# A sliding-window attention layer with a gated FFN on one core: two of four token blocks transposed through DRAM and VectorE, FFN tiles placed between the QKV blocks

## The chip, the cores and the metric

The kernel runs on one core of a Trainium2 chip. The metric is the device time of one execution in microseconds (us); for the kernel before it is 230.87 us, the median of 3 runs (230.71 to 231.08). All times below come from one profiled execution of that kernel, which took 230.75 us, and whose recorded span from the first to the last instruction is 229.0 us.

## The reference

```python
def reference(A_x, A_wqkv, A_wo, B_x, B_w_gate, B_w_up, B_w_down):
    x = A_x                                  # 1 x 2048 x 512, bf16
    xn = _layernorm(x, axis=-1)              # no scale, no shift
    s = _A_ref(xn, A_wqkv, A_wo)             # attention: 32 heads of 16; each token sees 8 keys,
                                             # its own and those 2, 4, ... 14 tokens back; then @ wo
    g = _silu(_B_ref(xn, B_w_gate, B_w_up, B_w_down))   # (gelu(xn @ w_gate) * (xn @ w_up)) @ w_down
    return x + s * g                         # FFN width 1792
```

## The kernel before

The 2048 tokens are 16 tiles of 128, in four blocks j of 512 (TQ). Everything stays on chip except V, which is written to DRAM transposed (`vT_dram`) and read back with shifted windows (`v_arr`). For each block the work is:

- `layer_norm` (L296 on): BatchNorm statistics on VectorE (L303, L304), the root on ScalarE (blocks 0 and 1, L310) or on GpSimd (blocks 2 and 3, L325 and L328), the normalised tile `xn_t` on VectorE (L335). `transpose` (L346 on) then turns each tile with four 128x128 TensorE transposes into PSUM (L351) and copies them to `xnT` (L359 on ScalarE, L361 on VectorE). `xnT` has the channels on the partitions and the tokens in a row: it is the moving operand of all that follows.
- `qkv` (L410 on): q, k and v, each four groups of four 128x512 matmuls over the channels (L430; block 0 in matmuls of 256 columns), evacuated by ScalarE (L443, L449, L454). The weights of q and k are read with a step of four elements.
- `scores` (L505 on): for each half w2 of the window, four products q * k on VectorE of 128x2048 (L517) and two pairwise sums (L527), then eight matmuls of 32 columns that sum over the head's channels (`L_ps`, L534), the exponential on ScalarE (L546), and the normaliser (`sum_ps` L588, reciprocal L598, `b_ps` L606).
- `values` (L623 on): the same on the V side (L639, L649, `O_ps` L656, `o_sb` L667).
- `ffn_pair` (L705 on), 14 a block: four matmuls for the gate and four for the up projection (both L710), gelu on ScalarE (L720), the product `hT` on VectorE (L727), which frees the bank of `u_ps`.
- `out_tile` (L744 on), 4 a block: 4 matmuls with wo (`s_ps`, L752), 14 with w_down (`y_ps`, L764), silu (L775), gate (L778), residual (L785), store (L789). The very last tile is cut only for the s part, in 384 and 128 columns.

The order on each engine is written by a small planner, the class `Order` (L45 to L151). Every piece of work is a task with an engine, an assumed duration (the constants L26 to L38), a priority, and the buffers that it takes and frees. `run` takes at each step the task that can start first, and emits it. The TensorE matmuls of qkv, ffn_pair and out_tile are one chain in the order of the loops at the end of the kernel (`add_main`, L391): all four qkv blocks, and then for each block 14 pairs and 4 output tiles. Transposes, score, sum and value matmuls go between them when their inputs are planned to be there.[...]

PSUM has four banks for the main chain (pool `psf`), two for transposes, scores and normalisers (`psa`) and one pair for `O_ps` (`pso`).

The loads are issued by SP (x, wqkv, in the order L195 to L216) and by ScalarE (w_gate, w_up, wo, w_down at L844, each behind a named task); the windows of V by GpSimd (L496).[...] `wqkv_sb` shares its buffer with the hidden tile `hT`.

Of the kernel before, what the change touches and what calls it, by code (L numbers as in the profile page):

```python
# [9 lines left out]
ALU = mybir.AluOpType  # L10
# [4 lines left out]
P = 128  # L15
# [9 lines left out]

MM = 0.216  # L26
COL16 = 1.1
COL8 = 0.65
TR = 0.28
PROD = 1.14  # L30
HMUL = 0.6
STATS = 0.8
NORM = 0.36
TRCOPY = 0.36
ACT1 = 0.62
ACT2 = 1.06
TABLE = 1.28
HOP = 0.2  # L38
# [6 lines left out]
class Order:  # L45
# [45 lines left out]
    def run(self):  # L91
        left = list(self.tasks)
        while left:
# [10 lines left out]
            if t.eng == "dve" and t.prio >= 1.0:  # L104
                soon = [
                    (self.ready(u), u.seq, u) for u in left
                    if u.eng == "dve" and u.prio <= -1.5 and self.ready(u) is not None
                ]
                if soon and min(soon)[0] < s + 0.4:
                    s, _, t = min(soon)  # L110
# [20 lines left out]
def kernel(  # L131
# [23 lines left out]
    def pool(name, bufs, **kw):  # L155
# [9 lines left out]
    prpool = pool("prpool", 6)  # L165
# [6 lines left out]
    psf = pool("psf", 4, space=bass.MemoryType.PSUM)  # L172
    psa = pool("psa", 2, space=bass.MemoryType.PSUM)
# [5 lines left out]
        {"xn": 4, "q": 3, "vst": 4, "va": 3, "pr": 6, "attn": 2, "o": 2, "h": 1, "gl": 3, "sg": 3,  # L179
         "f": 4, "a": 2, "O": 1}  # L180
# [5 lines left out]
    wqkv_sb = hpool.tile([P, 3, NC * D + 64], BF16, name="wqkv_sb", tag="h")  # L186
    order.taken["h"].append("wqkv")
# [3 lines left out]
    wd_sb = wpool.tile([P, NF, D], BF16, name="wd_sb")  # L191
    wqkv_v = A_wqkv.rearrange("(k p) n -> p k n", p=P)

    for t in range(TPB):
        eng = nc.sync if t % 2 == 0 else nc.scalar  # L195
        eng.dma_start(out=x_sb[:, t, :], in_=x2d[t * P : (t + 1) * P, :])  # L196
# [12 lines left out]
    load_wqkv(0)  # L209
# [6 lines left out]
    x_there = [3.2, 3.5, 3.8, 4.1] + [9.5] * 2 + [12.0] * 2 + [13.5] * 4 + [16.0] * 4  # L216
# [58 lines left out]
    xnT = cpool.tile([P, NC, S], BF16, name="xnT")  # L275
# [20 lines left out]
    def layer_norm(j):  # L296
# [49 lines left out]
        def transpose(t, dep, on_act):  # L346
            def fn():
                tiles["tr", t] = psa.tile([P, NC * P], BF16, name="tr_ps", tag="a")
                for c in range(NC):
                    cs = slice(c * P, (c + 1) * P)  # L350
                    nc.tensor.transpose(tiles["tr", t][:, cs], tiles["xn", t][:, cs], ident[:])  # L351
                if t < 2:
                    warm_up(2 + t, TQ // 2)
# [9 lines left out]
            a = add("pe", TR, fn, deps=[dep], prio=-1.0, takes=[("a", ("tr", t))], frees=[("xn", t)])  # L363
# [3 lines left out]
            )  # L367

# [8 lines left out]
        elif j == 1:  # L377
# [5 lines left out]
        else:  # L383
            r = rstd_done[j] = rstd_pool(ts[0], TPB, [stat(t) for t in ts])
            for t in ts:
                transpose(t, norm(t, r), on_act=False)
# [10 lines left out]
    v_stored = {}  # L397

# [11 lines left out]
    def qkv(j):  # L410
# [4 lines left out]
        for lo in range(0, TQ, n):  # L415
            for which in range(3):
                for c in range(0, NC, w):
                    key = (j, which, c, lo)

                    def mms(key=key, which=which, c=c, lo=lo):  # L420
                        ps = psf.tile([P, TQ], F32, name="qkv_ps", tag="f")
                        tiles["qkv", key] = ps
                        for i in range(w):
                            for dk in range(NC):
# [3 lines left out]
                                else:  # L428
# [4 lines left out]
                                    rhs=xnT[:, dk, j * TQ + lo : j * TQ + lo + n],  # L433
# [41 lines left out]
                    else:  # L475
                        st = add("sp", 0.6, store_v(j, c, lo, n, w), deps=[e], prio=-1.0)

                        v_stored[j] = add(
                            ("dma", key), 3.0, lambda: None, deps=[(st, 0.0)], frees=[("vst", key)]
# [5 lines left out]
    def load_values(j, half):  # L485
# [12 lines left out]
        issue = add("pool", 2.4, fn, deps=[v_stored[j]], prio=-2.0, takes=[("va", (j, half))])  # L498
        v_ready[j, half] = add(("dma", "va", j, half), 7.5, lambda: None, deps=[(issue, 0.0)])
# [5 lines left out]
    def scores(j, prio):  # L505
        exps = []
        for w2 in range(2):
# [21 lines left out]
            def reduce(w2=w2, prods=prods):  # L529
                L = psa.tile([P, TQ], F32, name="L_ps", tag="a")  # L530
                tiles["L", j, w2] = L
                for i in range(2):
                    for w4 in range(4):
# [5 lines left out]
                            stop=(i == 1),  # L539
# [14 lines left out]
            for c in range(NC):  # L554
# [9 lines left out]
                if c % 2 == 1:  # L564
# [3 lines left out]
                            opens=key, closes=key if last else None, frees=[("pr", (*key, c))],  # L568
                        )
                    )  # L570
            r = add(
                "pe", COL8, reduce, deps=[ps[-1]], prio=-0.5, takes=[("a", ("L", j, w2))],
                frees=[("pr", (*key, c)) for c in (0, 2)],
# [44 lines left out]
        s = add("pe", 0.4, sums, deps=[(e, 0.3) for e in exps], prio=-0.4, takes=[("a", ("sum", j))])  # L618
        r = add("dve", 1.15, recip, deps=[s], prio=-1.5, frees=[("a", ("sum", j))])
        b = add("pe", 0.3, spread_back, deps=[r], prio=-0.4, takes=[("a", ("b", j))])  # L620
        b_ready[j] = add("act", ACT1, b_copy, deps=[b], prio=-0.6, frees=[("a", ("b", j))])

    def values(j, prio):  # L623
# [10 lines left out]
        for half in range(2):  # L634
# [39 lines left out]
            for i in range(4):  # L674
# [19 lines left out]
                "pe", COL8, reduce, deps=[ps[-1]], prio=-0.5, takes=[("O", (j, half))],  # L694
# [10 lines left out]
    def ffn_pair(j, fc):  # L705
        def matmuls(w, name):
            ps = psf.tile([P, TQ], F32, name=name, tag="f")
            tiles[name, j, fc] = ps
            for dk in range(NC):
# [3 lines left out]
                    rhs=xnT[:, dk, j * TQ : (j + 1) * TQ],  # L713
# [10 lines left out]
        def mult():  # L724
            if fc == 0:
                tiles["h", j] = hpool.tile([P, NF, TQ], BF16, name="hT", tag="h")
            nc.vector.tensor_tensor(  # L727
                out=tiles["h", j][:, fc, :], in0=tiles["gl", j, fc][:], in1=tiles["u_ps", j, fc][:],
                op=ALU.mult,
            )  # L730
# [7 lines left out]
        h_ready[j, fc] = add(  # L738
            "dve", HMUL, mult, deps=[a, u], prio=-2.0, takes=[("h", j)] if fc == 0 else [],
            frees=[("f", ("u", j, fc)), ("gl", (j, fc))],  # L740
        )


    def out_tile(j, tt, split):  # L744
        t = j * TPB + tt
        last = tt == TPB - 1

# [12 lines left out]
        def y_mms(lo, hi):  # L760
            if lo == 0:
                tiles["y", t] = psf.tile([P, D], F32, name="y_ps", tag="f")
            for fc in range(lo, hi):
                nc.tensor.matmul(  # L764
                    tiles["y", t][:],
                    lhsT=tiles["h", j][:, fc, tt * P : (tt + 1) * P],
                    rhs=wd_sb[:, fc, :],
# [4 lines left out]
        def silu():  # L772
            tiles["sil", t] = fpool.tile([P, D], BF16, name="sil")
            tiles["sg", t] = fpool.tile([P, D], BF16, name="sg")
# [132 lines left out]
```

The softmax here doesn't subtract the row's maximum and nothing guards it: scores larger than these inputs give would overflow.

## Time and profile before

| What | Time or share |
|---|---|
| Median of 3 runs | 230.87 us |
| The profiled execution, its span | 230.75 us, 229.0 us |
| TensorE (PE) busy | 222.1 us, 97% of the span |
| VectorE (DVE) busy | 193.4 us, 84% |
| ScalarE (ACT) busy | 111.1 us, 49% |
| GpSimd (POOL) busy | 28.3 us, 12% |
| First qkv matmul starts, last s matmul ends | 7.68 us, 224.67 us |
| Granted TensorE clock | 0.998 |

A row of the profile's groups gives line, engine, operation, tiles and shape, then the number of instructions, the busy time and the mean duration of one. Matmuls overlap in the array, so a group's mean (380 ns for 512 columns) is longer than the spacing at which they follow each other: 44 qkv matmuls take 6.94 us in the chain, 24 of them with 256 columns. The chain of waits is read backwards from the last instruction; where TensorE is never idle, its pieces add up to the time.

### The profile page before, as it was taken

What the parts mean: (1) busy time and instruction counts of PE and PEld (TensorE: products, weight loads), DVE (VectorE), ACT (ScalarE), POOL (GpSimd) and SP (SyncE); (2) the same over time, 40 slices, a digit from 0 to 9 for tenths busy, and PEclk for the clock granted to TensorE, in tenths of its full rate; (3) what the DMA queues carried; (4) which work ended last, traced back from release to release, by engine and by line L of the source; (5) the groups of instructions that cost most, each with busy time, mean ns of one, the idle gap of its engine ahead of it and who ended that gap; (6) DMA issues with size and microseconds to landing.
All of it is one profiled execution on the core that took longest, in us unless ns stands there. A gap on an engine that the chain in (4) does not pass through costs nothing.

```text
span 229.0 us, 3272 instructions
## 1 busy us (share of the span) xinstructions
PE 222.1 (97%) x1234; PEld 104.8 (46%) x1234; DVE 193.4 (84%) x270; ACT 111.1 (49%) x167; POOL 28.3 (12%) x67
## 2 busy tenths in 40 slices
PE   7899999999999999999999999999999999999992
PEld 2796554354444444444444444444444344444441
DVE  4899999999999999999999999999759997342322
ACT  3576568477634365464445374434563164334211
POOL 7102930400412000040400002100000000000000
PEclk9999999999999999999999999999999999999999
DMA  5994799599718000054520011900000100000010
GB/s 172 342 384 163 166 207 375 163 296 336 185 32 186 3 0 23 23 141 94 134 54 3 0 46 28 207 0 0 1 3 23 46 24 0 3 0 0 23 46 25
DMA packets 15072, 22.64 MB, mean 99 GB/s; under 512 B 1472, under 2 KB 11984, under 8 KB 15056
## 3 DMA queue, kind: packets, MB, share of 16 engines
q0 software_dynamic: 2592, 8.54, 16.8%
q1 hardware_dynamic: 8592, 7.57, 10.5%
q10 hardware_dynamic: 3872, 6.32, 7.8%
q8 instruction: 9, 0.15, 0.3%
q14 instruction: 7, 0.06, 0.1%
HBM read 18.22 MB, written 4.21 MB: 98 GB/s over the span
## 4 chain that ended last, share of the span: by engine, by line
PE 88%; DMA 9%; DVE 1%; SPq 0%; ACT 0%; ACTq 0%; issue 0%; DVEq 0%
PE g_ps L710 21%; PE u_ps L710 21%; PE y_ps L764 21%; PE qkv_ps L430 12%; DMA wu_sb<-in_B_w_up_dram 7%; PE s_ps L752 6%; DMA wqkv_sb<-in_A_wqkv_dram 3%; PE O_ps L656 2%; PE L_ps L534 1%; PE tr_ps L351 1%; PE sum_ps L588 0%; PE b_ps L606 0%; SPq L196 0%; DVE sg L778 0%; ACT vst L454 0%; DVE sg L785 0%
## 5 line engine op out<-in xcount | busy, mean ns | idle before, releaser
L710 PE MATMUL g_ps<-xnT,wg_sb 128*128 128x512 bf16 x224 | 57.6, 380 | 0.0
L710 PE MATMUL u_ps<-xnT,wu_sb 128*128 128x512 bf16 x224 | 57.6, 380 | 0.0
L720 ACT ACTIVATE gl<-g_ps 128x512 bf16<-128x512 f32 x56 | 33.4, 597 | 48.8 <-PE g_ps L710 48.7
L764 PE MATMUL y_ps<-wd_sb,hT 128*128 128x512 bf16 x224 | 51.3, 380 | 0.0
L727 DVE TENSOR_TENSOR hT<-gl,u_ps 128x512 bf16<-128x512 bf16 x56 | 38.0, 683 | 12.5 <-PE u_ps L710 12.4
L430 PE MATMUL qkv_ps<-xnT,wqkv_sb 128*128 128x512 bf16 (+1 forms) x240 | 43.9, 337 | 1.1 <-DMA wqkv_sb<-in_A_wqkv_dram 0.6
L639 DVE TENSOR_TENSOR pv<-attn,v_arr 128x2048 bf16<-128x2048 bf16 x32 | 38.4, 1219 | 0.1
L517 DVE TENSOR_TENSOR prod<-q_sb,k_sb 128x2048 bf16<-128x2048 bf16 x32 | 38.3, 1219 | 0.0
L710 PEld LDWEIGHTS <-wg_sb 128*128 128x128 bf16 x224 | 21.4, 98 | 27.6 <-issue 2.5
L710 PEld LDWEIGHTS <-wu_sb 128*128 128x128 bf16 x224 | 21.6, 98 | 27.2 <-issue 1.7
L764 PEld LDWEIGHTS <-hT 128*128 128x128 bf16 x224 | 21.5, 98 | 25.7 <-issue 0.4
L430 PEld LDWEIGHTS <-wqkv_sb 128*128 128x128 bf16 x240 | 24.9, 108 | 16.5 <-issue 1.3
L496 POOL DMA_DIRECT2D v_arr<-vT_dram x32 | 18.7, 590 | 100.9 <-DVE pv L639 86.7
L775 ACT ACTIVATE sil<-y_ps 128x512 bf16<-128x512 f32 x16 | 9.6, 597 | 33.2 <-PE y_ps L764 33.1
L778 DVE TENSOR_TENSOR sg<-sil,s_ps 128x512 bf16<-128x512 bf16 (+2 forms) x17 | 11.1, 653 | 11.5 <-PE s_ps L752 7.7
L527 DVE TENSOR_TENSOR prod<-prod 128x2048 bf16<-128x2048 bf16 x16 | 19.5, 1221 | 0.2
L649 DVE TENSOR_TENSOR pv<-pv 128x2048 bf16<-128x2048 bf16 x16 | 19.5, 1220 | 0.2
L752 PE MATMUL s_ps<-wo_sb,o_sb 128*128 128x512 bf16 (+2 forms) x68 | 16.5, 367 | 0.0
L303 DVE BATCH_NORM_STATS2 stats<-x_sb 128x6 f32<-128x512 bf16 x16 | 10.8, 673 | 2.0 <-DMA x_sb<-in_A_x_dram 2.0
L454 ACT ACTIVATE vst<-qkv_ps 128x512 bf16<-128x512 f32 x16 | 9.4, 600 | 6.3 <-PE qkv_ps L430 3.1
L443 ACT ACTIVATE q_sb<-qkv_ps 128x512 bf16<-128x512 f32 x16 | 9.5, 604 | 4.8 <-PE qkv_ps L430 4.8
L449 ACT ACTIVATE k_sb<-qkv_ps 128x512 bf16<-128x512 f32 x16 | 9.2, 598 | 3.9 <-PE qkv_ps L430 3.9
(56 smaller groups left out, 121.1 us busy)
## 6 DMA issues: line engine op xcount, KB each, us to landing
v_arr<-vT_dram POOLq DMA_DIRECT2D x32, 260.0 KB, 5.2
vT_dram<-vst SPq DMA_DIRECT2D x16, 128.0 KB, 6.0
out_dram<-sg SPq DMA_DIRECT2D x15, 128.0 KB, 1.7
wg_sb<-in_B_w_gate_dram ACTq DMA_DIRECT2D x1, 1792.0 KB, 9.3
wu_sb<-in_B_w_up_dram ACTq DMA_DIRECT2D x1, 1792.0 KB, 15.0
wd_sb<-in_B_w_down_dram ACTq DMA_DIRECT2D x1, 1792.0 KB, 10.0
wqkv_sb<-in_A_wqkv_dram SPq DMA_DIRECT2D x3, 512.0 KB, 6.9
x_sb<-in_A_x_dram SPq DMA_DIRECT2D x2, 512.0 KB, 8.9
```

The costliest lines, as they stand in the source:

```text
L430: nc.tensor.matmul(ps[:, i * n : (i + 1) * n], lhsT=wqkv_sb[:, which, ws], rhs=xnT[:, dk, j * TQ + lo : j * TQ + lo + n], start=(dk == 0), ...
L496: nc.gpsimd.dma_start(out=v_arr[32 * w4 : 32 * (w4 + 1), :, :], in_=src)
L517: nc.vector.tensor_tensor(out=prod[:], in0=tiles["q", j][:, c, :].unsqueeze(1).to_broadcast([P, 4, TQ]), in1=kwin, op=ALU.mult,)
L527: nc.vector.tensor_tensor(out=a[:], in0=a[:], in1=b[:], op=ALU.add)
L639: nc.vector.tensor_tensor(out=pv[:], in0=tiles["attn", j][:, w2, :].unsqueeze(1).to_broadcast([P, 4, TQ]), in1=tiles["va", j, half][:, 4 * ...
L649: nc.vector.tensor_tensor(out=a[:], in0=a[:], in1=b[:], op=ALU.add)
L710: nc.tensor.matmul(ps[:], lhsT=w[:, dk, fc * P : (fc + 1) * P], rhs=xnT[:, dk, j * TQ : (j + 1) * TQ], start=(dk == 0), stop=(dk == NC - 1),)
L720: nc.scalar.activation(out=tiles["gl", j, fc][:], in_=tiles["g_ps", j, fc][:], func=AF.Gelu_apprx_tanh)
L727: nc.vector.tensor_tensor(out=tiles["h", j][:, fc, :], in0=tiles["gl", j, fc][:], in1=tiles["u_ps", j, fc][:], op=ALU.mult,)
L752: nc.tensor.matmul(tiles["s", t][:, cs], lhsT=tiles["o", j][:, c, tt * P : (tt + 1) * P], rhs=wo_sb[:, c, cs], start=(c == 0), stop=(c == ...
L764: nc.tensor.matmul(tiles["y", t][:], lhsT=tiles["h", j][:, fc, tt * P : (tt + 1) * P], rhs=wd_sb[:, fc, :], start=(fc == 0), stop=(fc == N ...
L778: nc.vector.tensor_tensor(out=tiles["sg", t][:, cs], in0=tiles["sil", t][:, cs], in1=tiles["s", t][:, cs], op=ALU.mult,)
```

## The change

1. Blocks 2 and 3 of `xn` no longer pass TensorE. `around` stores each normalised tile to DRAM (four DMAs of 128 KB a block, on SP), reads the block back with tokens spread over partitions in 32-row pieces (four DMAs of 128 KB in runs of 256 bytes, on SP), and turns it with two VectorE 32x32 transposes on pairs of bf16 channels taken as one 32-bit element. The result `xnT2` holds the two channels of a pair side by side, so the moving operand of all qkv and FFN matmuls of blocks 2 and 3 has a step of two elements (4 bytes). To fit this, the channel order is changed everywhere: a partition holds four neighbouring channels (`(p k)` in place of `(k p)`), and the TensorE transposes of blocks 0 and 1 read every fourth column.
2. The roots of blocks 2 and 3 move from GpSimd to ScalarE, in pairs of tiles.
3. The main chain has 5 FFN pairs of block 0 behind qkv block 1, and 4 behind qkv block 2.
4. w_gate and w_up are loaded in halves (columns 0 to 895, then the rest); the first halves at the place of the old w_gate load, the second behind q of block 2. w_down takes over the buffer of wqkv and is loaded behind the last v.
5. The q weights are loaded in two halves on SP and ScalarE ahead of x tiles 2 and 3.
6. In block 3 the scores' two pairwise sums are added on VectorE (one 128x2048 add more for each half of the window), and TensorE sums with four matmuls in place of eight.
7. The last tile's y, s, silu, gate, residual and store go in halves of 256 columns; the first half's residual is on GpSimd.
8. The planner's durations, priorities and look-ahead have other values, and so the order on every engine changes.

```diff
+G = dict(
+    MM=0.217, COL8=0.568, COL4=0.2, TR=0.28, PROD=1.167, HMUL=0.672, HMUL2=0.34, STATS=0.873,
...
+    xget=6.735, vst=2.654, vload=6.3, vissue=2.706, TURN=1.815, x2=13.724, x3=19.121, FULL=(3,),
+    UPACT=(), BETWEEN={1: 5, 2: 4}, NPE=2, trig=[0, 0, 3, 3], s_prio=[1.0, 2.0, 3.0, 4.0],
+    v_prio=[1.5, 2.0, 3.75, 4.5], e_lat=0.206, b_lat=0.1, p_sum=-1.5, p_red=-0.5, p_tr=-1.0,
+    p_h=-1.4, wo_at=0, fb=4, ab=2, ob=1, prb=6, x_early=[3.2, 3.5, 3.8, 4.1],
+)
...
-    wqkv_sb = hpool.tile([P, 3, NC * D + 64], BF16, name="wqkv_sb", tag="h")
-    order.taken["h"].append("wqkv")
+    wqkv_sb = wpool.tile([P, 3, NC * D + 64], BF16, name="wqkv_sb", tag="wd")
...
-    wqkv_v = A_wqkv.rearrange("(k p) n -> p k n", p=P)
+    wqkv_v = A_wqkv.rearrange("(p k) n -> p k n", p=P)
...
-    load_wqkv(0)
+    load_tile(0, nc.sync)
+    load_tile(1, nc.scalar)
+    load_q(0, 2, nc.sync)
+    load_q(2, 4, nc.scalar)
+    load_tile(2, nc.sync)
+    load_tile(3, nc.sync)
     load_wqkv(1)
...
+    def xn_cols(j, dk, lo, n):
+        at = j * TQ + lo
+        if j < NPE:
+            return xnT[:, dk, at : at + n]
+        at -= NPE * TQ
+        return xnT2[:, dk // 2, at : at + n, dk % 2]
...
-                    cs = slice(c * P, (c + 1) * P)
-                    nc.tensor.transpose(tiles["tr", t][:, cs], tiles["xn", t][:, cs], ident[:])
-                if t < 2:
-                    warm_up(2 + t, TQ // 2)
+                    nc.tensor.transpose(
+                        tiles["tr", t][:, c * P : (c + 1) * P], tiles["xn", t][:, c::NC], ident[:]
+                    )
+                if t == 1:
+                    warm_up(3, TQ // 2)
...
+        def around(j, normed):
...
+            x_dram = dram.tile([TQ, D], BF16, name=f"xn_dram{j}")
...
+                    nc.sync.dma_start(out=x_dram[i * P : (i + 1) * P, :], in_=tiles["xn", ts[0] + i][:])
...
+                for b in range(4):
+                    src = bass.AP(
+                        tensor=x_dram.tensor, offset=x_dram.offset + b * P,
+                        ap=[[D, 32], [32 * D, 4 * TPB], [1, P]],
+                    )
+                    nc.sync.dma_start(out=xr[32 * b : 32 * (b + 1), :, :], in_=src)
...
+                for i in range(2):
+                    nc.vector.transpose(
+                        out=xnT2[:, i, at : at + TQ, :].bitcast(F32),
+                        in_=tiles["xr", j][:].bitcast(F32)[:, :, i::2],
+                    )
...
-                                    rhs=xnT[:, dk, j * TQ + lo : j * TQ + lo + n],
+                                    rhs=xn_cols(j, dk, lo, n),
...
-                for i in range(2):
+                for i in range(1 if full else 2):
...
+            def whole(prods=prods):
+                a, b = prods[0], prods[2]
+                nc.vector.tensor_tensor(out=a[:], in0=a[:], in1=b[:], op=ALU.add)
...
+        columns = [slice(0, D)] if not split else [slice(0, D // 2), slice(D // 2, D)]
...
-        edges = (0, D) if not split else (0, D - P, D)
...
+            on_pool = split and not end
             d = add(
-                "dve", 0.06 + 0.31 * (cs.stop - cs.start) / D, lambda cs=cs: residual(cs), deps=[d],
+                "pool" if on_pool else "dve", 0.06 + 0.31 * part(cs),
+                lambda cs=cs, e=nc.gpsimd if on_pool else nc.vector: residual(cs, e), deps=[d],
...
-        start(wg_sb[:], B_w_gate.rearrange("(k p) n -> p k n", p=P), copied[2])
-        start(wu_sb[:], B_w_up.rearrange("(k p) n -> p k n", p=P), k_ready[1])
+        half = DF // 2
+        when = [copied[2], q_ready[1], k_ready[1], q_ready[2], k_ready[2], q_ready[3], k_ready[0]]
+        for n, (w_sb, w) in enumerate(((wg_sb, B_w_gate), (wu_sb, B_w_up), (wg_sb, B_w_gate), (wu_sb, B_w_up))):
+            lo = n // 2 * half
+            start(
+                w_sb[:, :, lo : lo + half],
+                w.rearrange("(p k) n -> p k n", p=P)[:, :, lo : lo + half], when[G["trig"][n]],
+            )
...
+        add("act", 0.5, down, deps=[v_last[NJ - 1]], prio=-3.0)
...
     for j in range(NJ):
         qkv(j)
+        if j in G["BETWEEN"]:
+            ffn_pairs(0, G["BETWEEN"][j])
```

## The prediction

> **What bounds the kernel now.** I read the page's busy times first, then TensorE's waits, the chain, the timeline of the places the change touches, and the groups. Columns of the waits: engine, line and who released it, us in total, times, longest. Of the chain: start, us, what. Of the timeline: start, us, engine, operation, idle time before.
>
> ```profile
> PE 222.1 (97%) x1234; PEld 104.8 (46%) x1234; DVE 193.4 (84%) x270; ACT 111.1 (49%) x167; POOL 28.3 (12%) x67
> ```
> ```profile
> PE warm_ps L285 <- DVE eps_sb L223: 1.2, 1, 1.2
> PE qkv_ps L430 <- DMA wqkv_sb<-in_A_wqkv_dram: 0.6, 1, 0.6
> PE qkv_ps L430 <- ACT vst L454: 0.5, 1, 0.5
> PE tr_ps L351 <- DVE xn_t L335: 0.2, 1, 0.2
> ```
> TensorE is the bound: from its first qkv matmul at 7.68 to the last at 224.67 us it waits once, 0.48 us. So the time falls by whatever leaves its list, and rises by every wait put in.
>
> ```profile
> 14.44 0.45 PE tr_ps L351 x8
> ...
> 24.01 0.45 PE tr_ps L351 x8
> ...
> 51.53 0.55 PE L_ps L534 x8
> ...
> 223.78 0.89 PE s_ps L752 x8
> 224.74 0.57 DVE sg L778
> 225.33 0.36 DVE sg L785
> 225.69 0.21 DVE sg L778
> 225.93 0.23 DVE sg L785
> ```
> These are prices on TensorE (two transposed tiles 0.45, one score sum 0.55) and the tail: 1.49 us of VectorE behind the last matmul.
>
> ```profile
> 27.54 0.38 ACTq L844 DMA_DIRECT2D wu_sb<-in_B_w_up_dram  x1
> ...
> 40.15 2.97 ACTq L844 DMA_DIRECT2D wo_sb<-in_A_wo_dram  x3
> 43.25 1.08 ACT L454 ACTIVATE vst<-qkv_ps 128x512 bf16<-128x512 f32 x2 [3.08 <-DMA wu_sb<-in_B_w_up_dram]
> ```
> The one wait's cause: ScalarE is held 3.08 us by a wo load whose semaphore is still w_up's, and so evacuates v late.
>
> [...]The new moving operand steps 4 bytes[...]. The trace shows no strided moving operand; its strided weights (8 bytes) are slower, below.[...] The trace's queues agree that small packets cost: SP's average 881 bytes at 45 ns, ScalarE's 1632 at 74 ns, so about 11 ns a packet + 0.039 ns a byte, and 256 bytes come to 21 ns.
>
> **Part by part, on TensorE's list.**
> - Transposes: blocks 2 and 3 are 8 tiles, four groups of 0.45: **-1.80**. Their 8 copies on VectorE (413 ns, 3.3 us) go too.
> - Block 3's score sums: four matmuls for eight, half of 0.55, twice: **-0.55**.
> - The vst wait:[...] nothing on ScalarE waits for w_up. **-0.48**. What is next late there: gate and up at FFN column tile 7.
> - Start: the first qkv waits for wq at 7.68, while `xnT` is ready at 7.19 (copy 6.76 + 0.43). With 256 KB less ahead of wq the start is at most 0.43 earlier (0.06 of hand-over); but wv landed at 3.27 + 8.2 = 11.5 against a need at 11.65, with the same bytes ahead as now. I take **-0.25**, ends 0 and -0.43.
> - Last tile: 28 matmuls of 256 columns by 0.109 (24 take 2.62 in the chain) are 3.06, for 14 x 0.216 = 3.02: 0. Tail: gate and residual of 256 columns are some 0.42 and 0.29 (between the rows of 128 and 384), 0.8 us for 1.49. GpSimd's residual is not shown; a 128x32 add takes 0.24 there[...]. **-0.6**, ends -0.2 and -0.75.
>
> - At nothing: the strided loads of the transposes' weights (14 ns more at most, beside the matmul before); two warm-up matmuls less (they stood in the wait for wq); four roots of 0.29 more on ScalarE, which is idle half of the time there (gone, they would delay a qkv evacuation by 0.3 each, and four banks cover that); w_gate and w_up in packets of 1792 bytes for 3584, 11 ns x 512 / 16 = 0.35 us each; the k weights, which landed at 2.2 + 6.9 = 9.1 and are wanted at 9.3.
>
> This is -3.68. Now what the additions put in, as waits of TensorE.
>
> **Round trip of block 2.** VectorE: the statistics reach this place at 16.2 us in the timeline; four of them (0.79), two copies (0.38) and twice a reciprocal with two normalisings (0.9) bring the block's last tile to 21.9. SP: its store goes at 22.4; a V store at this hour landed in about 2.2 us (its evacuation ended at 20.33 and GpSimd began the loads that wait for it at 23.0; the median of all is 6.0): 24.6. The four reads queue on SP behind the first store of block 3, whose tile is ready at 24.1, and are issued from 24.6 to 26.4. The block is 2048 packets x 21 ns / 16 engines = 2.7 us of all engines, but V windows go beside it, so I use their landing, median 5.2 (3.7 to 9.4): 31.6. VectorE comes to its transposes at 33.7, held by the second FFN pair (29.6 + 2 x 1.73, then hT 0.6). What TensorE wants next is the first score sum at 38.25: qkv of blocks 0 and 1 end at 7.43 + 96 x 0.109 + 6 tiles x 0.225 + 48 x 0.216 = 29.6, and 5 pairs are 8.65. Between lie two transposes (512 elements each.[...] a PSUM product of 512 takes 0.68[...]. I take 0.8), one hT (0.6) and one add (1.2). So they have to start by 34.85: 3.2 us after the data. Queued behind them on VectorE are that hT, which frees a bank of `u_ps`, and the sum; TensorE waits for both. Block 3's reads, some 5 us later, are needed 18 us later.
>
> **Weights.** The old w_gate landed at 10.76 + 9.3 = 20.1; as many bytes are now both first halves, needed at 29.6. The second halves go behind q of block 2, at 43.3; with the same 9.3 they land at 52.6, and column tile 7 wants them at 53.9 (38.25, a score sum 0.66 with its change-over, qkv 10.37, a sum 0.66, two pairs 3.46, normaliser 0.45). w_down goes behind the last v: 53.9 + 3.46 + 10.37 + two sums 1.32 + evacuation 0.8 = 69.8, and took 10.0 in full queues: 79.8, against a need at 79.2 (five pairs, a value sum and the s matmuls behind 69.0). This is the thinnest cover: 0 to 0.6.
>
> **VectorE.** It gains 2 adds of 1.22 and 4 transposes (3.2) and loses copies (3.3): +2.3 on 193.4. From the end of block 0's values (73.5) to block 3's last it has 68 operations of 2048 by 1.15 (1.13 apart when alternating with others, 1.25 for a dependent one), 43 hT by 0.61, 12 gates with residuals by 1.06 and 8.7 of normalisers: 126 us. TensorE has there 19.9 for the rest of block 0, twice 39.7 for blocks 1 and 2, 20.7 for 12 pairs, and 7.9 of sums: 128. So VectorE keeps pace, but each deadline is close, and hT, which was put first till now, queues behind products. ScalarE gets 5 more table loads of 1.28 and stays near 52%; four banks cover one load. For all new waits together I take **+0.4**, ends 0 and 3.
>
> Sum: -1.80 - 0.55 - 0.48 - 0.25 - 0.6 + 0.4 = -3.28. The profiled execution took 230.75 (span 229.0 and 1.75 around): 227.5. The median of the runs is 0.12 higher: **227.6 us**. With all terms at their good ends it is 226.9, with new waits of 3 us 230.2.
>
> **Rivals.**
> - The interleaved operand is slow; this case ends slower than before. 320 matmuls (96 qkv, 224 gate and up) read `xnT2`. For it: weights of q and k at 8-byte steps load slower, 112 ns in the median below where contiguous ones take 98, 14% more.[...] It decides from (3.28 + 0.46) / 320 = 12 ns a matmul; at 14% of 0.216 it is 30 ns, 9.7 us in all: **237.3**.
> ```profile
> L430 PEld LDWEIGHTS <-wqkv_sb x240: 95/112/132, 7.7 to 55.0; 128*128 128x128 bf16 x120
> ```
> - The round trip is late and holds VectorE. Stores at 6.0 (28.4), issue 1.8 and reads at 9.4 land it at 39.6, 4.8 behind 34.85, and TensorE sees all of it: **232.4**. For it: the DMA share in the row of 28 to 43 us below. Against: w_up's 1.8 MB, a good part of that row, are loaded elsewhere now.
> - VectorE paces the middle: its 2 us over 128 are used up, and the freed TensorE time comes back as waits for sums and hT, the full 3 us: **230.2 to 230.7**, no change. Against: it idles 4.4 us in the second row below. Columns: stretch, us, busy time of each engine, clock, DMA share, GB/s.
> ```profile
> 28.00:43.00 15.00, 15.00 (x90) 7.37 (x92) 14.90 (x21) 8.85 (x15) 2.42 (x2) 1.00 0.95 271
> ...
> 141.00:184.00 43.00, 43.00 (x230) 18.51 (x229) 38.59 (x47) 19.76 (x28) 2.31 (x4) 1.00 0.17 41
> ```
>
> **How the numbers follow.** About 0.2% is what a measurement can tell from no change. Forecast 0.70; slow operand 0.12; late round trip 0.08, a quarter of it late by so little that it ends at no change; VectorE pacing 0.10, of which 0.02 stays faster, 0.06 is no change and 0.02 slower. So faster 0.72, same 0.08, slower 0.20. The forecast's own range is 226.9 to 230.2. The whole range is 226.5 to 231.2: 0.4 below for the rounding of eight terms, and above it takes in VectorE pacing and small sizes of the two others, whose full sizes are what is left out.
>
> **What would show it.** Right: qkv and FFN matmuls of blocks 2 and 3 spaced 0.216 in the chain, no transposes after 19 us, TensorE waits under 1 us, last s matmul at about 222.0, VectorE's end under 1 us behind. Wrong: spacing above 0.228; a wait of VectorE for the read-back beyond 1 us; TensorE waits for hT, L or w_down that add up to 3.

## The result, and the profile after

The kernel after takes **244.57 us** (median of 4 runs, 243.06 to 244.75) where the kernel before took 230.98 beside it: 1.0575 times as long, 95% interval 1.0531 to 1.0618. The forecast was 227.6 with a range up to 231.2: wrong in sign. The profiled execution took 244.65 us, with a span of 242.9. A run more than 1.5% above the fastest of its kernel counts as slow, and the comparisons rest on the others (this concerns e12, e14 and one run of e7 below).

The page of the kernel after: busy times, then the granted clock and the DMA engines' busy share in 40 slices of 6.07 us (9 is full or nearly).

```profile
PE 228.4 (94%) x1206; PEld 104.9 (43%) x1206; DVE 196.9 (81%) x271; ACT 118.5 (49%) x177; POOL 24.7 (10%) x64
...
PEclk9999998599999986999999999999999999999999
DMA  6995997999009980010446101007000100000010
```
TensorE has fewer instructions than before (1206 for 1234) and is busy longer. The clock, 0.998 before, is 0.971 in the mean, and it dips twice. The DMA engines are nearly full from 24 to 61 us (busy share 0.98) and from 73 to 91 (0.99), ahead of and around the dips. TensorE's waits in the kernel after (in the form that the prediction explains):

```profile
PE y_ps L872 <- DMA wd_sb<-in_B_w_down_dram: 4.2, 1, 4.2
PE L_ps L610 <- DVE prod L603: 3.4, 1, 3.4
PE warm_ps L310 <- DVE eps_sb L237: 1.3, 1, 1.3
PE tr_ps L375 <- DVE xn_t L360: 0.5, 1, 0.5
PE qkv_ps L504 <- DVE xnT L387: 0.2, 1, 0.2
```
Two new waits stand where the prediction had allowed 0.4 us in all. The chain of the kernel after shows what each ends on and what comes behind it:

```profile
27.42 11.72 DMA xr<-xn_dram
...
39.96 0.67 DVE xnT L429
40.63 0.57 DVE hT L826
41.20 1.14 DVE prod L603
42.39 0.62 PE L_ps L610 x3
43.00 12.34 PE qkv_ps L504 x44
...
66.73 8.29 PE qkv_ps L504 x36
...
76.62 14.28 DMA wd_sb<-in_B_w_down_dram
90.94 6.99 PE y_ps L872 x21
...
118.56 0.86 PE g_ps L799 x4
...
136.27 4.53 PE y_ps L872 x21
...
159.84 0.91 PE g_ps L799 x4
...
238.15 0.76 DVE sg L889 x2
238.94 0.58 DVE sg L896
```
VectorE's wait for the read-back, and the issue of its four loads on SP (timeline):

```profile
39.33 1.30 DVE L429 STREAM_TRANSPOSE xnT<-xr 128x512 f32<-128x512 f32 x2 [5.07 <-DMA xr<-xn_dram]
```
```profile
25.32 6.15 SPq L421 DMA_DIRECT2D xr<-xn_dram  x4
```
Four things are to be read from these:

1. The last load of the read-back (`xr`) took 11.7 us from the start of its issue and ends at 39.1. Its issue alone held SP for 4.05 us, from 27.42 to 31.47; in e12 below, where the windows come later, the same four issues take 2.16 us together. VectorE waits 5.1 us for the data; the turns, a product hT and a sum follow, and TensorE waits 3.4 us in the middle of block 0's first score sum. (The expectation of e2 calls it block 2's; block 2's qkv starts only behind it, at 43.0.)
2. w_down took 14.3 us, and the first y starts 4.2 us late.
3. Behind each wait TensorE is slow. 21 matmuls of y take 6.99 us at 90.94 and 4.53 at 136.27: 2.45 lost. Behind the first wait 44 qkv matmuls take 12.34 us; at the 0.230 of block 3 (8.29 / 36) they would take 10.1: 2.2 lost.
4. Four gate or up matmuls on the interleaved operand (159.84) take 0.906 us, on the contiguous one (118.56) 0.863, as means over ten or eleven such groups in a row: 11 ns each. In qkv it is 0.230 for 0.216, 14 ns. 224 x 11 + 96 x 14 ns are 3.8 us.

The last s matmul ends at 238.08, predicted at 222.0: 16.1 later. 3.4 + 2.2 + 4.2 + 2.45 + 3.8 are 16.05. Of that, 0.4 had been allowed for waits within the 222.0, so some 0.4 are left for small terms (the start 0.08 later than forecast, block 3's two score sums 0.11). The stretches of the two clock dips in the kernel after (columns: stretch, us, busy time of PE, PEld, DVE, ACT, POOL, clock, DMA share, GB/s):

```profile
84.00:92.00 8.00, 3.78 (x16) 1.48 (x15) 7.30 (x8) 1.88 (x2) 0.00 (x0) 0.80 0.80 173
92.00:100.00 8.00, 8.00 (x35) 2.98 (x34) 2.85 (x4) 3.34 (x4) 0.00 (x0) 0.78 0.06 18
44.00:50.00 6.00, 6.00 (x20) 2.33 (x19) 4.03 (x7) 2.39 (x4) 1.39 (x3) 0.68 1.08 201
```

What fills the DMA engines while the read-back is out, in the kernel after from 22 to 40 us (queue: packets, MB, share of the 16 engines; q0 is GpSimd's, which carries the V windows, q1 is SP's, with the read-back):

```profile
q0 software_dynamic: 640, 2.13, 56.6%
q1 hardware_dynamic: 3483, 1.77, 43.1%
```
Together 99.7%, and more than half of it is windows that are first used at about 60 us.

**Theory.** Four causes: the read-back late, w_down late (both because V windows use the DMA engines at that time), the interleaved operand slower, and a lower clock behind each long wait. **Rivals**, one for each: VectorE's own pace makes the score sum late; packets of 256 bytes, and 1.8 MB, take that long anyway; the matmuls of blocks 2 and 3 are slow through traffic or clock; the clock is low through the load. In the trace the granted clock is 0.50 from 41.0 to 47.8 us and from 88.8 to 95.6: 6.8 us each, begun 2.0 us after TensorE stopped, with 5.4 and 4.7 us of it behind the wait. An estimate from that, half of these, is 2.7 and 2.3 us lost; the trace lost 2.2 and 2.45. The prediction counted no lower clock.

### The profile page after: what moved, and what is told of

Same layout as the page of the kernel before. It is cut to its first block, busy times and chain, and to the rows that moved or that the text cites. A ratio compares the mean times of both kernels' runs of the same rounds, so it can differ in the third digit from the quotient of the medians.

```text
span 242.9 us, 3257 instructions
## 1 busy us (share of the span) xinstructions
PE 228.4 (94%) x1206; PEld 104.9 (43%) x1206; DVE 196.9 (81%) x271; ACT 118.5 (49%) x177; POOL 24.7 (10%) x64
## 3 DMA queue, kind: packets, MB, share of 16 engines
q0 software_dynamic: 2592, 8.54, 16.6%
## 4 chain that ended last, share of the span: by engine, by line
PE 75%; DMA 14%; DVE 7%; SPq 2%; issue 1%; DVEq 0%; ACT 0%
PE y_ps L872 21%; PE g_ps L799 17%; PE u_ps L799 17%; PE qkv_ps L504 10%; DMA wd_sb<-in_B_w_down_dram 6%; PE s_ps L860 5%; DMA xr<-xn_dram 5%; DMA x_sb<-in_A_x_dram 3%; DVE stats L328 2%; PE L_ps L610 2%; PE O_ps L745 2%; DVE xn_t L360 1%; SPq L421 1%; DVE xnT L387 1%; DVE mv L329 1%
## 5 line engine op out<-in xcount | busy, mean ns | idle before, releaser
L799 PE MATMUL g_ps<-xnT,wg_sb 128*128 128x512 bf16 x224 | 58.7, 384 | 0.0
L799 PE MATMUL u_ps<-xnT,wu_sb 128*128 128x512 bf16 x224 | 58.7, 384 | 0.0
L872 PE MATMUL y_ps<-wd_sb,hT 128*128 128x512 bf16 (+1 forms) x238 | 53.2, 379 | 4.2 <-DMA wd_sb<-in_B_w_down_dram 4.2
L504 PE MATMUL qkv_ps<-xnT,wqkv_sb 128*128 128x512 bf16 (+1 forms) x240 | 46.8, 352 | 0.2 <-DVE xnT L387 0.2
L872 PEld LDWEIGHTS <-hT 128*128 128x128 bf16 x238 | 23.3, 100 | 31.4 <-DMA wd_sb<-in_B_w_down_dram 4.7
L884 ACT ACTIVATE sil<-y_ps 128x512 bf16<-128x512 f32 (+1 forms) x17 | 9.7, 572 | 43.4 <-PE y_ps L872 43.3
L889 DVE TENSOR_TENSOR sg<-sil,s_ps 128x512 bf16<-128x512 bf16 (+1 forms) x17 | 11.0, 652 | 17.3 <-ACT sil L884 9.5
L860 PE MATMUL s_ps<-wo_sb,o_sb 128*128 128x512 bf16 (+1 forms) x68 | 16.4, 367 | 0.0
## 6 DMA issues: line engine op xcount, KB each, us to landing
wd_sb<-in_B_w_down_dram ACTq DMA_DIRECT2D x1, 1792.0 KB, 14.3
```

The lines of the kernel that those rows point to most:

```text
L504: nc.tensor.matmul(ps[:, i * n : (i + 1) * n], lhsT=wqkv_sb[:, which, ws], rhs=xn_cols(j, dk, lo, n), start=(dk == 0), stop=(dk == NC - 1),)
L799: nc.tensor.matmul(ps[:], lhsT=w[:, dk, fc * P : (fc + 1) * P], rhs=xn_cols(j, dk, 0, TQ), start=(dk == 0), stop=(dk == NC - 1),)
L860: nc.tensor.matmul(tiles["s", t][:, cs], lhsT=tiles["o", j][:, c, tt * P : (tt + 1) * P], rhs=wo_sb[:, c, cs], start=(c == 0), stop=(c == ...
L872: nc.tensor.matmul(tiles["y", t, cs.start][:], lhsT=tiles["h", j][:, fc, tt * P : (tt + 1) * P], rhs=tiles["wd"][:, fc, cs], start=(fc == ...
```

## The experiments

The diffs are shortened: long names and arguments are left out, and comments are added.

### The operand: e4, e3, e10

e4 is the kernel before with the copy's output in pairs:

```diff
-o = xnT[:, :, t * P : (t + 1) * P]
+o = xnT2[:, :, at : at + P, :].rearrange("p a n b -> p a b n")   # blocks 2 and 3
```


> Kernel before, with the transposed activations of blocks 2 and 3 copied from PSUM into pairs (channel tiles 0 and 1 side by side, and 2 and 3), so that the same 320 matmuls as in the kernel after read every second bf16; nothing else changes but the copy's output step. My theory: 224 x 11 ns + 96 x 13 ns: 231.0 + 3.7 = 234.7, gate and up of blocks 2 and 3 at 0.91 a group of four, of blocks 0 and 1 at 0.86. Rival (operand costs nothing): 231.0 to 231.4.

Measured: **234.85** (ratio 1.015, 1.0103 to 1.0197), clock 1.00. In its chain a group of four reads so in blocks 2 and 3:

```profile
212.45 0.91 PE u_ps L724 x4
```
Nothing else of the change is in this kernel, so the operand's price is shown: 3.5 us over the runs beside it (231.36). (Its copies into pairs are slower too, 0.59 us for 0.41 in the mean, on VectorE; TensorE's waits for transposes grow by 0.8 us, while its wait for v is gone.)

e3 is the kernel after with four turns of bf16 a block into a contiguous tile:

```diff
-for i in range(2): nc.vector.transpose(out=xnT2[:, i, at : at + TQ, :].bitcast(F32),
-                                       in_=xr[:].bitcast(F32)[:, :, i::2])
+for i in range(NC): nc.vector.transpose(out=xnT[:, i, j * TQ : (j + 1) * TQ], in_=xr[:, :, i::NC])
```


> Kernel after, with each block turned by four 32x32 turns of bf16 instead of two of pairs of bf16 taken as fp32, so that the operand of blocks 2 and 3 lies contiguous, as in blocks 0 and 1; the round trip, the order and w_down stay. My theory: the 320 matmuls lose 11 to 14 ns each, 3.7 us in all; four turns of 512 elements may take 1.4 us more a block, of which block 2's would be seen: 240.9 to 242.3. Spacing of gate and up in blocks 2 and 3 back to 0.86 a group of four. Rival (the operand costs nothing, those matmuls are slow by the traffic or the clock of their time): spacing stays 0.91, 244.6 to 246.

Measured: **242.55**, 2.0 less than after, 0.25 outside what I expected. The spacing is back (0.86), but four turns take 2.49 us where two took 1.30, and the wait for the score sum grew from 3.4 to 4.4.

e10 asks how the price grows with the step:

```diff
-return xnT2[:, dk // 2, at : at + n, dk % 2]
+return xnT2[:, at : at + n, dk]          # the four channel tiles of a token side by side
```


> Kernel before, with the transposed activations of blocks 2 and 3 in fours (all four channel tiles of a token side by side), so that the same 320 matmuls read every fourth bf16, 8 bytes apart; with every second (4 bytes) it was 234.85. If a gap costs as much per byte of step, three times the extra of 4 bytes beyond 2: 231.1 + 3 x 3.7 = 242; if in proportion to the elements skipped a doubling, 238.5; if any step costs the same 11 ns (my theory: a fixed price for a step), 234.9. The copies' output step is larger too, on VectorE, which has room.

Measured: **307.65**; all three guesses were wrong. From its chain, in block 3:

```profile
283.83 1.81 PE u_ps L723 x4
285.64 0.86 PE s_ps L765 x4
```
At a step of 8 bytes a matmul takes 0.452 us for 0.216, at a mean clock of 0.997; the s matmuls beside it take 0.216. Its copies into `xnT2` became slower too (1.2 us for 0.41, in the turn of a block), but 320 x 0.236 = 75.5 us is nearly the whole difference of 76.3. So here 4 bytes cost 5 to 7% (227 and 230 ns for 216) and 8 bytes 109%: neither free nor in proportion.

### The clock: e8

The kernel after, with TensorE kept busy while it waits for w_down:

```diff
 tiles["y", t, cs.start] = psf.tile(...)
+if t == 0:
+    for _ in range(18):
+        nc.tensor.matmul(y, lhsT=warm[:, 0:P], rhs=warm[:], start=True, stop=True)
```


> Kernel after, with 18 matmuls of zeros into the first y bank ahead of the first y (3.9 us of TensorE, while it waits 4.2 us for w_down); the first real matmul of y starts the bank anew, so the result is the same. My theory: TensorE is not idle, its clock is not lowered afterwards, and the first 21 matmuls of y take 4.5 instead of 7.0 us: 244.6 - 2.45 = 242.1. Rival: the clock is lowered for another reason (traffic, the work of that stage), 244.6; or the dummies hold up y: 245 or more.

Measured: **242.11**. Its wait at y is 0.7 and the 21 matmuls behind it take 4.69:

```profile
76.41 14.64 DMA wd_sb<-in_B_w_down_dram
91.09 4.69 PE y_ps L877 x21
```
w_down is as late as before, the traffic is the same, and the clock of the two stretches from 84 to 100 us is 1.00 (0.80 and 0.78 in the kernel after). So this dip came from idleness, not from load, and cost 2.3 to 2.5 us. Waits of 2.9 us (e2) to 5.9 (e6) were followed by a dip; single waits of 1.2 (e7 and e11, clock 1.00) and 1.6 (e14, groups of four at 0.86 behind it) were not. In e5, below, two of 1.7 and 0.6 close together were (clock 0.90 from 85 to 100 us).

A wait's length doesn't tell how long the dip is. In the kernel after the clock changes at 40.97, 47.80, 88.76 and 95.59 us: the two dips last 6.83 us each, with 40.96 between them. In the other kernels the mean clock of the stretches, taken as time at 0.50, gives an estimate of 3.3 us in e1, 6.8 in e2, 3.4 and 6.9 in e3 and 6.9 in e6. A wait of 2.9 us brought 6.8 us in e2, one of 4.4 brought 3.4 in e3. What decides between the two isn't shown, as no run varies this alone. The loss was 1.6 us in e1 (44 qkv matmuls in 11.71 us, for 10.1) and up to 2.45 in the kernel after (21 matmuls of y in 6.99, for 4.53).

### w_down: e1, e13

e1 loads it in pieces as the q, k and v weights come free:

```diff
-tiles["wd"] = wpool.tile([P, NF, D], BF16, name="wd_sb", tag="wd")     # behind v_last[3]
+start(wd0_sb[:], wd_v[:, 0:2, :], q_ready[3])                          # a buffer of its own
+for i, d in enumerate((q_ready[3], k_ready[3], v_last[3])):            # the places of q, k, v
+    add("act", 0.5, down(i), deps=[d], prio=-3.0)
```


> Kernel after, with w_down in four pieces: two of its 14 column tiles in a buffer of their own, and three times four in the places of the q, k and v weights, each loaded as soon as block 3 has no more use for that weight. Nothing else is moved. My theory (four causes: late round trip, interleaved operand, late w_down, and a lower granted clock behind each long wait): the last piece is 512 KB, not 1.8 MB, and is wanted 10.1 + 10 x 0.216 = 12.3 us after its issue, so the wait of 4.2 us at the first y goes, and with it the 2.45 us by which the first 21 matmuls of y ran slow: 244.6 - 6.6 = 238.0 us. Rival: the DMA engines are full of V windows there whatever the pieces, the last piece is as late as the whole was (14.3 us), TensorE waits about 2 us inside the first y and the clock falls all the same: 242 to 243.

Measured: **236.63**, 7.9 less than after; no wait at y, clock 0.992. That is more than the 6.65 of this wait and its clock: the first wait was shorter too (3.1), with some 3.3 us of low clock behind it (from the stretches' means) instead of 6.8, so y's turn came at 85.2 for 86.7. e13 leaves the load whole and moves what runs beside it:

```diff
+if (j, half) == (1, 1):
+    nc.gpsimd.tensor_copy(out=seen[:, 0:1], in_=tiles["wd"][:, NF - 1, 0:1])   # then the windows
```


> Kernel after, with the V windows of block 1's second half and of all later ones held until w_down has landed (GpSimd copies one column of w_down ahead of them); the order on every other engine is unchanged. My theory (w_down was late because windows shared the DMA engines with it): it takes about 10 us as in the kernel before, lands at 86 to 87, and the wait of 4.2 and the 2.45 of low clock behind it are gone or nearly: 238 to 239. Rival (1.8 MB behind the last v are late whatever runs beside them): it takes 13 us or more and the wait stays over 3: 243.5 to 244.6.

Measured: **236.83**. The DMA issues of e13 (KB each, us to landing):

```profile
wd_sb<-in_B_w_down_dram ACTq DMA_DIRECT2D x1, 1792.0 KB, 8.0
```
8.0 us for 14.3 (10.0 in the kernel before), and no wait at y. The windows of V made w_down late; that is now shown. (By the mean clock, 0.990 for 0.992 in e1 and 0.971 in the kernel after, the first dip is the short one here too, and y's turn came 0.5 us earlier.)

### The read-back: e2, e6, e12, e14

e2 takes the round trip out, e6 gives it time:

```diff
-... NPE=2, ...
+... NPE=4, ...                               # e2: TensorE turns all four blocks
-xget=6.735, ... BETWEEN={1: 5, 2: 4}, ...
+xget=12.5, ... BETWEEN={1: 7, 2: 2}, ...     # e6
```


> Kernel after, with all four blocks turned by TensorE (the number of blocks that it turns set from 2 to 4): no DRAM round trip, no 32x32 turns, contiguous operand everywhere; the q halves, the last tile in halves, FFN tiles between QKV blocks, the split weights and the late w_down stay. My theory: the wait of 3.4 us for block 2's score sum goes, with the 2.85 us of low clock behind it, and so do the 320 x 11.5 ns of the interleaved operand (3.7); 8 tiles' transposes come back (1.8): 244.6 - 8.2 = 236.4, with w_down still late by 4.2. Rival: the wait at the score sum was VectorE's own pace, and its 8 copies (3.3 us) keep it late by 2 to 3 us: 239 to 240. Second rival: the clock is low because of the kernel's load and not behind waits, and stays at 0.97: 239.

Measured: **235.55**, 0.85 below the number, but not by the way I gave: no wait for the score sum, none for w_down, and a new one in its place.

```profile
PE O_ps L745 <- DVE pv L738: 2.9, 1, 2.9
```
Block 0's values end on VectorE at 84.45 us, behind score products of block 1 and the copies that are back; TensorE wants them at 81.6. A dip (clock 0.59 from 84 to 92 us) follows, so the first of the rivals was partly right.

> Kernel after, with two numbers of its planner changed: the read-back is planned at 12.5 us instead of 6.7, and seven FFN tiles lie between QKV blocks 1 and 2 and two between 2 and 3, instead of five and four. The turns then stand behind block 0's score work on VectorE. Nothing else. My theory: the wait of 3.4 us and the 2.85 us of low clock behind it go; TensorE reaches QKV of block 2 at about 42.2, 1 us after the turns end at 41: 244.6 - 6.2 = 238.4, with w_down late and the operand slow as before. Rival: the wait returns elsewhere, since the score products behind the turns are late too, or w_down's wait grows by what is won: 241 to 244.

Measured: **240.39**, below the rival's 241 and 2 above mine. The wait for the score sum fell to 0.5, but w_down, issued 4.6 us earlier in the same traffic, took 16.6 us, and its wait grew from 4.2 to 5.9.

e12 and e14 move the competing windows of block 0, with every other engine's order as it was:

```diff
+nc.gpsimd.tensor_copy(out=seen[:, half : half + 1], in_=tiles["xr", 2][:, 0, 0:1])   # e12
+nc.gpsimd.tensor_copy(out=seen[:, 0:1], in_=xr[:, 0, 0:1])    # e14: xr of block 3; then the windows
```


> Kernel after, with the V windows of block 0 (8 loads of 260 KB, issued at 22.8 us beside the read-back) made to wait for the read-back of block 2: GpSimd copies one column of it ahead of each half's loads. Nothing else changes; the windows are first used at about 60. My theory (the read-back was late because it shared the DMA engines with the windows): it lands at 31 to 33 for 39.3, VectorE's wait of 5.1 goes, and so do TensorE's 3.4 and the 2.85 of low clock: 238 to 239. Rival (packets of 256 bytes, four reads on one queue and w_gate's and w_up's loads are enough): it lands at 36 or later, 242 to 244.6.

Measured: **241.8**, the mean of 240.22 and 243.32. Two runs 3 us apart, between my time and the rival's, decide nothing; the trace, of the run of 243.32, shows the mechanism as I had it. GpSimd saw block 2's read-back at 30.1 us (39.1 in the kernel after), and VectorE didn't wait for it. But the windows then ran beside block 3's read-back, whose last load took 12.2 us, and VectorE's list has that turn ahead of block 0's score products (timelines of GpSimd and of VectorE in e12):

```profile
30.14 1.07 POOL L567 COPY seen<-xr 128x1 bf16<-128x1 bf16 x1 [23.04 <-DMA xr<-xn_dram]
```
```profile
33.95 1.30 DVE L431 STREAM_TRANSPOSE xnT<-xr 128x512 f32<-128x512 f32 x2
...
44.99 1.30 DVE L431 STREAM_TRANSPOSE xnT<-xr 128x512 f32<-128x512 f32 x2 [5.71 <-DMA xr<-xn_dram]
```
TensorE's wait for a score sum is still 2.9. In e14 the windows go behind both:

> Kernel after, with the V windows of block 0 held until the read-backs of both blocks have landed; the order on every other engine is unchanged. With the windows held for block 2's read-back alone, that one landed at 30.1 and the wait moved to block 3's, which then shared the engines with the windows. My theory: both land within 5 us of their issue, VectorE never waits for them, the first wait of TensorE (3.4) and its low clock (2.85) go: 244.6 - 6.2 = 238.4, w_down and operand as before. Rival: the windows, now at 36 to 48, collide with the second halves of gate and up or are late themselves at 57 to 60: 241 or more.

Measured: **243.04** (single runs 241.65, 243.04 and 243.34): the rival's time. Both read-backs land in 3.1 us (median; 7.7 in the kernel after), and VectorE never waits for them. The waits of TensorE in e14 say who is late now:

```profile
PE y_ps L878 <- DMA wd_sb<-in_B_w_down_dram: 3.9, 1, 3.9
PE g_ps L805 <- ACT vst L534: 2.6, 1, 2.6
PE u_ps L805 <- DMA wu_sb<-in_B_w_up_dram: 1.6, 1, 1.6
```
The second half of w_up, issued at 43.6 into the held windows, takes 17.6 us in e14's chain. The DMA engines have hardly any room in this stretch (0.98 busy from 24 to 61 us in the kernel after), so in both kernels what was put off made the next transfer late.

### What is left: e5, e7, e9, e11, e15

e5 has the small parts alone in the new planner settings (NPE=4, BETWEEN={}), e11 in the order of the kernel before (its diff: q weights in halves, `for i in range(1 if full else 2)` in the score sum, one add more):

> Kernel after, with all four blocks turned by TensorE and no FFN tiles between QKV blocks, so that of the change only its small parts are left: q weights in halves, block 3's score sums of four matmuls, gate and up weights in halves behind other triggers, w_down after the last v, the last tile in halves. My theory: block 3's sums 0.55, the one wait of the kernel before 0.48, the start 0.25 (first qkv at 7.5 for 7.68), the tail next to nothing (its end was 1.44 us behind the last matmul, 1.49 before): 231.0 - 1.3 = 229.7. w_down has 14 pairs (24 us) to land and is not late; the clock stays at 1.00. Rival: the parts cost waits of their own, or the two added sums make VectorE late, and nothing is left: 231.0 or more.

Measured: **234.93**, 5 above my number: the planner's new settings, with TensorE's transposes, end block 0's values at 83.2 us (69.1 in the kernel before), and TensorE waits for them (1.7, and 0.6 behind), with a dip. The small parts can't be read from it.

> Kernel before with two small parts of the change alone, in its own order: q weights in halves with tiles 2 and 3 behind them, and block 3's score sums of four matmuls with one more add each. My theory: the first qkv starts 0.3 earlier (7.3 to 7.5 in the kernels with halves, 7.68 before) and two sums of 0.33 stand for two of 0.55, 0.44: 231.1 - 0.7 = 230.4. Rival: the added adds make VectorE late, or another wait takes the gain: 231.1 or more.

Measured: **230.27** (ratio 0.9952, 0.9935 to 0.997): faster, by half a percent. Together the start and the sums give what was expected, though in its profile the wait for the v evacuation grew from 0.5 to 1.2. e15 is e11 with wo's loads behind q of block 3:

```diff
-start(wo_sb[32 * e : 32 * (e + 1), :, :], v[e], k_ready[2])
+start(wo_sb[32 * e : 32 * (e + 1), :, :], v[e], q_ready[3])
```


> Kernel before with the q weights in halves and block 3's sums of four (230.27 alone), and wo's four loads issued behind q of block 3 instead of k of block 2. There TensorE's one wait in the middle (1.2 us for a v evacuation, whose engine is held by a wo load that waits for w_up's semaphore) was what was left. My theory: w_up has landed by then, the wait goes: 230.3 - 1.2 = 229.1. Rival: the held load only moves, or wo's bytes collide with w_down's: 230.3.

Measured: **230.85** (ratio 0.9979, 0.9969 to 0.999). The wait went, as I said; the time didn't fall. The planner had moved VectorE's work with it, and the chain of e15 runs through VectorE from 113 to 132 us.

e7 mends all three (the edits of e1, e3 and e6 together); e9 is e7 with the last tile as in the kernel before:

```diff
-columns = [slice(0, D)] if not split else [slice(0, D // 2), slice(D // 2, D)]
+columns = [slice(0, D)] if not split else [slice(0, D - P), slice(D - P, D)]   # s only; y whole
-on_pool = split and not end
+on_pool = False
```


> Kernel after, with all three mended: w_down in pieces, turns of bf16 into a contiguous operand, and the read-back planned at its real length with seven and two FFN tiles between. My theory: 236.6 (with the pieces alone) less 3.1 (wait), 1.7 (clock behind it) and 3.7 (operand): 228.1, which is faster than the kernel before by 1.2%, by about the 1.8 us of transposes and the small parts. Rival: turns of 2.5 us a block and the late read-back make VectorE pace the middle: 231 or more.

> The kernel with all three mended, with the last tile as in the kernel before: y in one bank of 512 columns, s in 384 and 128, everything on VectorE. From the last matmul to the end of the span the kernel before took 4.33 us, the kernel after 4.82 and the mended one 4.86, so my theory is that the halves with GpSimd cost 0.5 us: 231.4 - 0.5 = 230.9, span's end 4.3 behind the last matmul. Rival: the end behind the last matmul is the store's and not the split's, 4.8 as before, 231.4.

Measured: e7 **231.42** (ratio 1.0019, 1.0001 to 1.0037; single runs from 230.4 to 235.0), which is the rival's number; e9 **230.48** (0.9964, 0.9945 to 0.9984). Thirteen of the 13.6 us are back with e7. The 0.9 between e7 and e9 is more than the 0.5 that the profiles show (from the last matmul to the end of the span 4.86 in e7, 4.38 in e9); the rest may be scatter. Why no 228? TensorE's listed waits in e9, the warm-up's apart, add up to 2.8 us for 1.3 in the kernel before; the longest, 1.2, is for VectorE in a normaliser. And in e9's chain the middle is VectorE's:

```profile
45.41 2.48 DVE xnT L425 x4
47.90 1.11 DVE prod L598
49.00 2.28 DVE prod L588 x2
51.31 1.23 DVE prod L598
52.53 2.28 DVE prod L588 x2
54.84 1.23 DVE prod L598
...
62.47 2.28 DVE pv L723 x2
64.78 1.22 DVE pv L733
66.00 2.28 DVE pv L723 x2
```
From 45 to 93 us it goes nearly all the way from product to product, with TensorE's deadlines just met or missed by little. That VectorE's pace is what keeps e9 from 228 is read from this chain; no run makes VectorE's work shorter.

| Kernel | Median, us | The one before beside it | Shows |
|---|---|---|---|
| e4, operand alone on before | 234.85 | 231.36 | operand +3.5 |
| e13 / e1, w_down mended | 236.83 / 236.63 | 231.49 / 231.36 | late w_down and dip, 7.7 to 7.9 of 13.6 |
| e8, no dip behind it | 242.11 | 231.12 | dip 2.4 |
| e9, all mended, old tail | 230.48 | 231.34 | nearly all is back; chain through VectorE |
| e11, small parts on before | 230.27 | 231.34 | fastest, with e9 |

## Why the prediction was wrong

Four terms of its sum failed: the landing of the read-back, the landing of w_down, the clock behind a wait, and the operand. They are 3.4, 4.2, 2.2 + 2.45, and 3.8 us of the 16.1.

- **"Round trip of block 2"** failed in its landing. The stores and the start of the issue were nearly right (25.3, predicted 24.6), the turns too (1.30 for 1.6, where 0.8 a turn was the author's estimate); the end of the issue was not (31.5, predicted 26.4). "So I use their landing, median 5.2" was wrong: the landing was 11.7. It was a median from another time of the kernel before. In e14, without the windows, it is 3.1 us, and in e12 block 2's is there at 30.1, so the 8 loads of 260 KB issued at 22.8 were the cause; the packet price (21 ns; 24.8 in the mean of the 4096 packets of 256 bytes in the trace of after) was not. The rival "late round trip" named a busy DMA as this cause and had 0.08. Its landing of 39.6 is near the 39.1 measured partly by luck: it took the stores to be slow, which they weren't, and the reads to take 9.4. Its sum of 232.4 lacked the clock and the other terms.
- **"Weights"**: w_down "took 10.0 in full queues" was carried to a place where it takes 14.3 beside windows and 8.0 without. I called this cover the thinnest and still let it count with the 0.4 for all new waits.
- **New waits "+0.4, ends 0 and 3"**: a wait was priced at its length. 3.4 and 4.2 us of waiting cost another 2.2 and 2.45 through the clock. This step was missing, and the first wait itself comes from the landing above.
- **The interleaved operand at nothing** was wrong: 3.8 us by the trace, 3.5 by e4. That it costs nothing was an assumption: the kernel before has no strided moving operand in its trace. The price lay just below the deciding 12 ns (11 and 14 measured), so this rival was right in kind, and at 30 ns too high in size. At a step of 4 bytes 5 to 7% is lost (227 and 230 ns for 216), at 8 bytes (e10) the matmul takes 2.1 times as long (452 ns).
- **Tail "-0.6"**: it became +0.5. VectorE's last residual takes 0.58 us beside GpSimd's 0.66 where 0.29 was reckoned, so VectorE ends 1.44 behind the last matmul (1.49 before), and from there to the span's end it is 3.4 for 2.8. The last store, of 256 columns for 128, is only 0.1 of that: 1.6 us from issue to landing for 1.5. The rest stays open.
- **"VectorE keeps pace"** couldn't show in the kernel after, where TensorE waits. Its rival (230.2 to 230.7) has the number that e9 gives, 230.48, once the other causes are gone, and the chain of e9 runs through VectorE; but e9's turns take 2.4 us more of VectorE than the forecast's, so the match in number is partly luck.
- Right: the start (7.51, predicted 7.43), the vst wait gone, gate's and up's second halves in time, block 3's sums (0.33 each for 0.275).

So what failed first is one kind of step twice: a transfer's length read from a row measured elsewhere (5.2 for 11.7, 10.0 for 14.3), though the windows stood in the list of the same stretch. The clock then added more than half as much again to each wait (2.2 to 3.4 us, 2.45 to 4.2). Left open: how much of e7's scatter is the DMA's, what the tail's missing 0.5 is, and whether a planner order exists in which the freed 3 us stay.

## What to carry to other kernels

Before a transfer is put on the critical path, add up what the other queues move in that stretch; a median landing from elsewhere says little (5.2 us for 11.7, 10.0 for 14.3 here), and moving one transfer out of a full stretch moved the wait (e12, e14). Price a long wait of TensorE above its length: in these kernels waits of 3.1 us (e1) and of 3.4 and 4.2 (after) lost another 1.6, 2.2 and 2.45 us through the clock, and 18 harmless matmuls in the last of them (e8) saved 2.4. A gain on the busiest engine is worth no more than the slack of the next one, here VectorE's.

## What the runs showed of the hardware

- A moving operand with a step of 4 bytes: 227 to 230 ns for 512 columns (after, e4); 8 bytes: 452 (e10); contiguous: 216.
- One 32x32 turn of a 128x512 tile: 0.69 us in fp32 pairs (after), 0.67 in bf16 (e3), as many elements in half the bytes.
- 18 matmuls of zeros where the kernel after waits 4.2 us kept the clock at 1.00 from 84 to 100 us (e8), where it was 0.80 and 0.78 (after).
- Low-clock stretches behind a wait: 6.83 us at 0.50, twice, behind 3.4 and 4.2 us (after); by estimate from the mean clock 3.3 us behind 3.1 (e1), 6.8 behind 2.9 (e2), 3.4 behind 4.4 (e3), 6.9 behind 5.9 (e6).
- A residual on VectorE (128x256) took 0.58 us beside one on GpSimd of 0.66 (after), 0.36 for 384 columns alone (before).
